# In step 1, one sum of two g blocks by VectorE instead of an accumulating transfer

## The chip, the cores and the metric

The kernel runs on one core of one Trainium2 chip. The metric is the device time of one execution in microseconds. TensorE (PE in the profile) multiplies matrices and writes to PSUM; VectorE (DVE), ScalarE (ACT) and GpSimd (POOL) work element by element; SyncE (SP) and GpSimd issue the transfers. Each engine runs its own instructions in the order in which the program lists them, and waits on semaphores for the others.

## The reference

Input: x of 8 x 4096 x 192, all float32. First a convolution along the sequence with 7 taps, whose weights are a softmax over 8 heads of 24 columns each. Then, for the 32768 rows, two matrix products with an activation between:

```python
h = x @ w_in                                   # 192 -> 2048
g = h * (1.0 / (1.0 + np.exp(-1.702 * h)))
return (g @ w_out).astype(np.float32)          # 2048 -> 192
```

## The kernel before

**Steps.** The rows are cut into 32 steps (`big`, 0 to 31) of 1024 rows: 512 of one batch and 512 of another. Step 0 (`first_step`) is a simple one that runs while the weights are still being prepared. Steps 1 to 31 run the same code: `hidden(big, 0, ...)` and `hidden(big, 1, ...)` compute the first product in two halves, `second(big, ...)` the second product. All of it is written out by hand; nothing is reordered by a scheduler.

**The first product.** Each half multiplies combinations of weight blocks by combinations of the convolved input in a scheme that needs fewer block products than the plain way (`TERMS`, 21 products). The results are combined by VectorE with `sum2` (line 642; one instruction for each half of a PSUM pair, shown as L644) and copied by ScalarE into the buffers k15 to k20. Then ScalarE applies the activation (`gelu`, line 619) and writes `g`. The last combination of a half is `k18 = k18 + sums` (line 746); the last gelu is made of it. `sums` is a pair of PSUM banks.

**g blocks and spots.** g holds 16 blocks of 128 x 1024 numbers, `block(r, j)`, 512 KB each. A `spot` (line 139) is a place for one such block: spots 0 and 1 lie in `osbs` (the output staging buffer), spots 2 to 4 in `room` (the space of k19, k20 and k18), spots 5 to 20 are the g blocks themselves. Blocks of r 0 and 1, spots 5 to 12, come from the first half of the first product, spots 13 to 20 from the second half.

**The second product.** It, too, uses a scheme with fewer block products, and so needs sums of g blocks. `sum_g` (line 929) makes one: either an add or subtract of VectorE (`add_up`, lines 389 to 393; the profile shows L391 for an add, L393 for a subtract), or, with "acc", a transfer issued by GpSimd that adds one spot to another on the way (line 932). `EARLY_G` (line 887) lists the sums that need only the first half's blocks. They are issued in four places (`early(0)` to `early(3)`, lines 692, 700, 715, 733) of the second half (`v` = 1). For spot 8 these are `(0, 5, "+", 6)` on VectorE, into spot 0, and `(8, 0, "acc")`, which adds spot 0 to spot 8; both stand in `early(2)`. `early(3)` holds `(2, 9, "-", 0)`; it stands behind the VectorE sums for k20 and k16 and ahead of the one for k18.

`PLAN` (line 891) is the order of the second product proper. "main" and "side" name a form of the weights, a spot and a target; "go" issues so many steps, each of three matmuls of the main product (column groups 0 to 2) and one of the side product (the fourth column group) (lines 972 to 981; the profile shows L956). "sum" and "acc" are `sum_g`, "seed" and "join" are copies and sums of the small results. Its beginning:

```python
("side", 13, 16, "k0"), ("main", 1, 5, "p2", 1), ("go", 4), ("sum", 14, 14, "-", 18),
("main", 16, 10, "p3", 0), ("go", 2), ("sum", 7, 8, "-", 7), ("go", 1), ("cross",), ("go", 1),
("main", 0, 14, "p0", 1), ("go", 1), ("sum", 5, 11, "-", 19), ("go", 1), ("seed", "p4", "p2", 1),
("go", 1), ("seed", "k1", "p3", 1), ("go", 1), ("sum", 8, 8, "-", 16), ("seed", "p5", "k1", 1),
("side", 19, 1, "k1"), ("acc", 14, 13), ("main", 18, 0, "p2", 0), ("go", 3), ("sum", 6, 8, "-", 6),
("go", 1), ("main", 5, 8, "p1", 0), ("go", 1), ("sum", 4, 5, "-", 10), ...
```

So sums 7, 8 and 6 read spot 8, and so does the fifth main product. The side product goes to `sides = (bx[1], bs[1], by[1])`, one PSUM bank for each third of its columns; `bs` is the pair that the first product calls `sums`.

**Work for later steps.** The convolution of later steps runs beside this. GpSimd adds taps (line 509) and makes the convolution sums (`sums_c`, line 523, shown as L391 and L393 on POOL); it also issues the accumulating transfers of g and of some taps (lines 932, 521), all in one queue. SyncE issues the loads of x (line 99), the transfers that copy conv_t across to the other half of the partitions (`cross`, line 530, shown as L532) and the stores.

In step 1 the second half of the first product carries some work that later steps don't have there: with `big` = 1 the convolution of step 2 is made late, partly in this half (`work`, `turn_next`).

Of the kernel before, what the change touches and what calls it, by code (L numbers as in the profile page):

```python
# [15 lines left out]
def kernel(  # L16
# [546 lines left out]
    def give(early, big):  # L563
        given[early] = big
        for what in waiting[early]:
            cross_now(early, *what)
        waiting[early].clear()
# [44 lines left out]
    def terms(big, v, slot, *ts, first=False):  # L612
        for t in ts:
            product1(slot, *TERMS[t], big, v, first)
            first = False
# [3 lines left out]
    def gelu(b, u, v, src):  # L619
        m, n = divmod(b, 2)  # L620
        i = 2 * (v * len(PAIRS) + PAIRS.index((m, u)))
        dst = g[:, i // NG, n, :, i % NG : i % NG + 2, :]
        if isinstance(src, list):
            for h in range(2):
                act.activation(  # L625
                    dst[:, :, h, :], src[h].rearrange("p (o t) -> p o t", o=2), AF.Gelu_apprx_sigmoid
                )
        else:
            act.activation(  # L629
                dst.rearrange("p o h t -> p h o t"),  # L630
                src.rearrange("p h (o t) -> p h o t", o=2),
                AF.Gelu_apprx_sigmoid,
            )
# [4 lines left out]
    def copy2(dst, src):  # L638
        for h in range(2):
            act.copy(bank(dst, h), bank(src, h))  # L640

    def sum2(op, dst, a, b):
        for h in range(2):
            op(*(bank(t, h) for t in (dst, a, b)))  # L644
# [6 lines left out]
    def hidden(big, v, x, z, y, sums, work, fetch, last=lambda: None):  # L651

        def pe(slot, *ts, first=False):
            terms(big, v, slot, *ts, first=first)

        def taps_at(n):
            for _ in range(0 if v else n):
                next_tap()  # L660

        def early(i):
            for item in EARLY_G[i] if v else ():
                sum_g(*item)


        if v:
            pe(z, 7, first=True)
            give(True, big)
        if v:  # L670
            pe(sums, 12)
            copy2(k15, sums)
            pe(x, 5, 17)
        else:
            pe(x, 5)
            pe(sums, 12)
            copy2(k15, sums)
            pe(x, 17)
            taps_at(1)
        gelu(B11, 0, v, x)  # L680
        if not v:
            pe(z, 7, first=True)
        pe(sums, 0)
        copy2(k16, sums)
        taps_at(2)
        last()
        def turn_next():
            if big + 2 < N_BIG:
                need(f"done {big + 1}")
                turn_x(big + 2)  # L690

        early(0)
        if not v:
            work(2.0 if big > 1 else 1.6)
        elif big == 1:
            work(3.2)

        pe(y, 6, 14, first=True)
        sum2(vec.tensor_sub, x, z, k15)
        early(1)  # L700
        if not v or big == 1:
            work(1.6 if big > 1 else 1.2)
        pe(sums, 13)
        copy2(k19, sums)
        pe(x, 2)
        copy2(k18, x)
        taps_at(2)
        pe(z, 11)
        pe(sums, 20, 10)
        sum2(vec.tensor_sub, k15, y, k19)  # L710
        gelu(B12, 0, v, sums)
        pe(x, 4)
        copy2(k20, x)
        sum2(vec.tensor_sub, k19, z, k19)
        early(2)
        if not v or big == 1:
            work(1.1)
        gelu(B22, 1, v, k19)
        gelu(B22, 0, v, k15)
        taps_at(2)  # L720
        pe(y, 8)
        pe(sums, 1, 9, first=True)
        pe(y, 15)
        if v and big == 1:
            turn_next()
        elif not v:
            work(2.2 if big > 1 else 1.1)
        sum2(vec.tensor_add, k20, k20, sums)
        sum2(vec.tensor_sub, k16, y, k16)
        gelu(B11, 1, v, k20)  # L730
        pe(x, 18)
        gelu(B21, 1, v, x)
        early(3)
        fetch()
        if not v:

            copy2(y, z)
        gelu(B21, 0, v, k16)
        if not v:
            work(1.2)  # L740
        if not v and big > 1:
            turn_next()
        pe(sums, 3, 19)
        if not v:
            work(0.7)
        sum2(vec.tensor_add, k18, k18, sums)
        return lambda: gelu(B12, 1, v, k18)
# [129 lines left out]
    def store(big, n, o=None, queues=(nc.sync,) * 3):  # L877
# [9 lines left out]
    EARLY_G = [  # L887
        [(6, 6, "-", 10)], [(1, 7, "-", 6), (1, 1, "-", 11)], [(0, 5, "+", 6), (8, 0, "acc")],
        [(2, 9, "-", 0)],
    ]  # L890
    PLAN = [
# [37 lines left out]
    def sum_g(dst, a, op, b=None):  # L929

        if op == "acc":
            nc.gpsimd.dma_start(out=spot(dst), in_=spot(a), accum_op=ALU.add)  # L932
        else:
            add_up(spot, dst, a, op, b)
# [3 lines left out]
    def second(big, bx, by, bs, final, last):  # L938
# [66 lines left out]
        )  # L1005
        for item in PLAN:
            ops[item[0]](*item[1:])
# [6 lines left out]
    def work(us):  # L1014
        while todo and todo[0][1] <= us + 0.2:
            us -= todo[0][1]
            todo.pop(0)[2]()

    def next_tap():
        if ready:  # L1020
            ready.pop(0)[2]()
            while ready and ready[0][1] == 0:
                ready.pop(0)[2]()

    def need(label):
        for q in (todo, ready):
            while any(item[0] == label for item in q):
                q.pop(0)[2]()
# [161 lines left out]
    def turn_x(big):  # L1190
        for c in range(NC):
            transpose_x(big, c)
        if big + 1 < N_BIG:
            load_x(big + 1)
# [5 lines left out]
    def fetch(big, v, slot):  # L1200

        need(f"first {big}")
        terms(big, v, slot, 16, first=True)
# [49 lines left out]
```

## Time and profile before

| | us |
|---|---|
| median of 3 runs | 2283.81 (2282.80 to 2284.13) |
| the profiled execution | 2282.62 |
| its span | 2280.6 |
| PE busy | 2267.5 (99%) |
| DVE busy | 1930.9 (85%) |
| ACT busy | 1558.3 (68%) |
| POOL busy | 839.4 (37%) |

The profile is of one execution. Its span runs from the first to the last instruction; the execution's own time is a little more. "L393" is line 393 of the kernel, and a line can be that of a helper that serves many callers. A row of the order of time gives start, duration, engine, line, operation, output, inputs, shapes and count, and in brackets how long the engine had been idle before and what ended that. The chain is the work that ended last, followed back from the end to what released each piece. Step 1's second product starts at about 134 us and step 2's first product at 174.5 us.

### The profile page before, as it was taken

To read this page: it belongs to the slowest core of one execution; us is meant where nothing else is said; L and a number is where in the kernel's file an instruction comes from. 1 tells how busy PE (TensorE), PEld (TensorE's weight loads), DVE (VectorE), ACT (ScalarE), POOL (GpSimd) and SP (SyncE) were. 2 spreads that over 40 slices of the span, in tenths; PEclk is the share of its full clock that TensorE was granted. 3 is DMA by queue.
4 is the path that set the end of the run, shared out by engine and by line. 5 is a ranking of instruction groups with operands and counts; after the bars stand their busy time and mean duration, and the time that the engine had idled before them with its cause. 6 is when DMAs were issued, how large, how long until landed. Compare 5 with 4: busy or idle time off the path is not lost.

```text
span 2280.6 us, 60969 instructions
## 1 busy us (share of the span) xinstructions
PE 2267.5 (99%) x25238; PEld 1196.6 (52%) x25238; DVE 1930.9 (85%) x2794; ACT 1558.3 (68%) x2959; POOL 839.4 (37%) x826
## 2 busy tenths in 40 slices
PE   9999999999999999999999999999999999999999
PEld 5345555555555555555555555555555555555556
DVE  8888888888888888888888888888888888888877
ACT  7657766667766677666776666776667766667754
POOL 0444342344432344424444234443244442344400
PEclk9999999999999999999999999999999999999999
DMA  8866566665567665666656666556756566664443
GB/s 188 155 133 137 114 123 126 126 139 115 110 126 143 124 130 113 127 131 125 137 115 118 126 133 134 119 109 126 143 119 135 111 129 130 123 141 85 91 99 71
DMA packets 269076, 283.94 MB, mean 125 GB/s; under 512 B 117888, under 2 KB 205952, under 8 KB 268672
## 3 DMA queue, kind: packets, MB, share of 16 engines
q0 software_dynamic: 56496, 148.86, 36.4%
q1 hardware_dynamic: 210656, 130.80, 25.4%
q8 instruction: 199, 3.26, 0.6%
q14 instruction: 77, 0.63, 0.1%
q10 hardware_dynamic: 1648, 0.39, 0.1%
HBM read 53.15 MB, written 25.17 MB: 34 GB/s over the span
## 4 chain that ended last, share of the span: by engine, by line
PE 96%; DVE 1%; DMA 1%; POOL 1%; ACT 1%; issue 0%; SPq 0%; DVEq 0%; POOLq 0%; ACTq 0%
PE slot L603 34%; PE slot L956 33%; PE sums L603 15%; PE sums L956 12%; PE slot L802 1%; DMA g<-g 1%; POOL conv_t L509 0%; DMA g<-osbs 0%; DVE conv_t L496 0%; POOL conv_t L393 0%; DVE xt L473 0%; DMA xin<-in_x_dram 0%; DVE w_in_s L391 0%; DVE osbs L874 0%; ACT w_form L435 0%
## 5 line engine op out<-in xcount | busy, mean ns | idle before, releaser
L603 PE MATMUL slot<-conv_t,w_in_s 64*128 64x512 f32 x3740 | 861.1, 591 | 0.6 <-DVE room L644 0.3
L956 PE MATMUL slot<-g,w_form 128*32 128x256 f32 x7024 | 710.3, 379 | 0.0
L603 PEld LDWEIGHTS slot<-conv_t,w_in_s 64*128 64x128 f32 x3740 | 371.4, 187 | 430.3 <-issue 355.0
L393 DVE TENSOR_TENSOR g<-g 128x1024 f32<-128x1024 f32 x372 | 450.1, 1237 | 9.6 <-DMA g<-osbs 6.2
L956 PEld LDWEIGHTS slot<-g,w_form 128*32 128x32 f32 x7024 | 373.0, 110 | 120.3
L603 PE MATMUL sums<-conv_t,w_in_s 64*128 64x512 f32 x1660 | 407.4, 589 | 0.5 <-DVE w_in_s L376 0.3
L981 ACT COPY room<-slot 32x256 f32<-32x256 f32 x434 | 159.4, 367 | 317.0 <-PE slot L956 315.8
L629 ACT ACTIVATE g<-room 128x1024 f32<-128x1024 f32 x310 | 326.0, 1078 | 66.9 <-DVE room L644 66.9
L956 PE MATMUL sums<-g,w_form 128*32 128x256 f32 x2648 | 368.7, 379 | 0.0
L956 PE MATMUL slot<-g,w_out_s 128*32 128x256 f32 x4080 | 320.2, 381 | 5.0 <-DVE g L393 5.0
L932 POOL DMA_DIRECT2D g<-g x124 | 106.3, 857 | 494.7 <-PE sums L956 153.9
L603 PEld LDWEIGHTS sums<-conv_t,w_in_s 64*128 64x128 f32 x1660 | 170.2, 187 | 188.1 <-issue 141.9
L509 POOL TENSOR_TENSOR conv_t<-conv_t,g 128x512 f32<-128x512 f32 x180 | 261.4, 1452 | 15.2 <-POOL conv_t L509 3.9
L521 POOL DMA_DIRECT2D g<-g x120 | 105.6, 880 | 428.5 <-PE slot L956 136.4
L640 ACT COPY room<-slot 128x512 f32<-128x512 f32 x434 | 231.7, 602 | 38.7 <-PE slot L603 38.7
L507 ACT ACTIVATE g<-xt,cw 128x512 f32<-128x512 f32 x360 | 248.8, 731 | 2.2
L956 PEld LDWEIGHTS slot<-g,w_out_s 128*32 128x32 f32 x4080 | 164.9, 110 | 138.1 <-ACT g L625 22.7
L625 ACT ACTIVATE g<-slot 128x512 f32<-128x512 f32 x334 | 180.9, 599 | 49.5 <-PE slot L603 28.8
L496 DVE SCALAR_TENSOR_TENSOR conv_t<-xt,cw,conv_t 128x512 f32<-128x512 f32 (+1 forms) x210 | 194.0, 924 | 10.6 <-ACT conv_t L494 5.9
L956 PEld LDWEIGHTS sums<-g,w_form 128*32 128x32 f32 x2648 | 177.9, 110 | 36.8
L393 POOL TENSOR_TENSOR conv_t<-conv_t 128x256 f32<-128x256 f32 x180 | 181.9, 1025 | 9.4
L981 ACT COPY room<-sums 32x256 f32<-32x256 f32 x217 | 79.6, 367 | 144.3 <-PE sums L956 142.6
(184 smaller groups left out, 2883.4 us busy)
## 6 DMA issues: line engine op xcount, KB each, us to landing
g<-g POOLq DMA_DIRECT2D x124, 512.0 KB, 5.8
xin<-in_x_dram SPq DMA_DIRECT2D x240, 180.0 KB, 4.4
conv_t<-conv_t SPq DMA_DIRECT2D x180, 192.0 KB, 3.2
g<-g POOLq DMA_DIRECT2D x120, 256.0 KB, 3.8
out_dram<-osbs SPq DMA_DIRECT2D x186, 128.0 KB, 4.9
g<-osbs POOLq DMA_DIRECT2D x31, 512.0 KB, 4.7
g<-room POOLq DMA_DIRECT2D x31, 512.0 KB, 5.3
conv_t<-g POOLq DMA_DIRECT2D x60, 256.0 KB, 4.7
```

Of the source, the lines that this page charges most:

```text
L393: eng.tensor_sub(v(dst), v(a), v(b))
L496: vec.scalar_tensor_tensor(out=dst, in0=src, scalar=tap, in1=dst, op0=ALU.mult, op1=ALU.add)
L507: act.mul(home, conv_src(big, c, k), cw[:, c, k : k + 1])
L509: nc.gpsimd.tensor_add(dst, dst, home)
L521: nc.gpsimd.dma_start(out=out, in_=src, accum_op=ALU.add)
L603: nc.tensor.matmul(slot[h], w_in_s[halves[h], a, v * P : (v + 1) * P], src, start=first, stop=True, skip_group_check=True,)
L625: act.activation(dst[:, :, h, :], src[h].rearrange("p (o t) -> p o t", o=2), AF.Gelu_apprx_sigmoid)
L629: act.activation(dst.rearrange("p o h t -> p h o t"), src.rearrange("p h (o t) -> p h o t", o=2), AF.Gelu_apprx_sigmoid,)
L640: act.copy(bank(dst, h), bank(src, h))
L932: nc.gpsimd.dma_start(out=spot(dst), in_=spot(a), accum_op=ALU.add)
L956: nc.tensor.matmul(dst, w, t, start=first, stop=last, skip_group_check=True)
L981: act.copy(to, d)
```

## The change

In step 1 alone, the "acc" of spot 8 leaves `early(2)`, and `early(3)` begins with an add of VectorE, `(8, 8, "+", 0)`, which computes the same sum. All other steps keep `EARLY_G`.

```diff
         def early(i):
-            for item in EARLY_G[i] if v else ():
+            for item in (EARLY_G if big > 1 else EARLY_G_1)[i] if v else ():
                 sum_g(*item)
...
     EARLY_G = [
         [(6, 6, "-", 10)], [(1, 7, "-", 6), (1, 1, "-", 11)], [(0, 5, "+", 6), (8, 0, "acc")],
         [(2, 9, "-", 0)],
     ]
+    EARLY_G_1 = EARLY_G[:2] + [EARLY_G[2][:1], [(8, 8, "+", 0)] + EARLY_G[3]]
```

## The prediction

> **What bounds the kernel now.** I read the page's first lines and its chain by engine, then who TensorE (PE) waited for, then the chain, the clock and each engine's order of time around the one large wait.
>
> ```profile
> PE 2267.5 (99%) x25238; PEld 1196.6 (52%) x25238; DVE 1930.9 (85%) x2794; ACT 1558.3 (68%) x2959; POOL 839.4 (37%) x826
> ...
> PE 96%; DVE 1%; DMA 1%; POOL 1%; ACT 1%; issue 0%; SPq 0%; DVEq 0%; POOLq 0%; ACTq 0%
> ```
>
> TensorE is busy for 99% of the span of 2280.6 us and carries 96% of the chain, so only what lets TensorE run earlier changes the time. Its waits over the whole span, the two largest after start-up:
>
> ```profile
> PE slot L956 <- DVE g L393: 5.0, 1, 5.0
> ...
> PE slot L603 <- DVE room L644: 0.3, 1, 0.3
> ```
>
> The columns are total, times, longest. One wait of 5.0 us stands out; from 165 us to the end the same view has no row, so whatever TensorE gains before 165 us reaches the end unless a new wait takes it. The chain around it (start, us, what):
>
> ```profile
> 132.31 2.35 POOL conv_t L393 x2
> 134.66 7.96 DMA g<-osbs
> ...
> 143.79 2.36 DVE g L393 x2
> ...
> 146.19 1.06 PE slot L956 x5
> ```
>
> "DMA g<-osbs" is the accumulating transfer that the diff removes from step 1. GpSimd (POOL) issues it at 134.66, behind its convolution sums; it lands 7.96 us later; only then can VectorE (DVE) run "sum 7 = 8 - 7", then sum 5, then sum 8, whose result TensorE's fifth main product reads. VectorE in order of time:
>
> ```profile
> 120.24 1.83 DVE L393 TENSOR_TENSOR osbs<-g 128x1024 f32<-128x1024 f32 x1
> 122.18 2.10 DVE L393 TENSOR_TENSOR osbs<-osbs,g 128x1024 f32<-128x1024 f32 x1
> ...
> 132.16 1.28 DVE L393 TENSOR_TENSOR room<-g,osbs 128x1024 f32<-128x1024 f32 x1
> 134.02 1.28 DVE L644 TENSOR_TENSOR room<-room,slot 128x512 f32<-128x512 f32 x2 [0.58 <-PE slot L603]
> 135.22 1.22 DVE L393 TENSOR_TENSOR g<-g 128x1024 f32<-128x1024 f32 x1
> 142.65 4.75 DVE L393 TENSOR_TENSOR g<-g 128x1024 f32<-128x1024 f32 x4 [6.21 <-DMA g<-osbs]
> ```
>
> The row at 132.16 is early sum (2, 9, "-", 0); the new add goes right ahead of it. 134.02 is the two halves of the k18 sum, 135.22 is sum 14, 142.65 is sums 7, 5, 8, 6. GpSimd's operations beside these (the first goes with VectorE's rows at 120.24 and 122.18, the second with the row at 132.16; a further one, alone, takes 0.73 from 133.98):
>
> ```profile
> 121.07 2.13 POOL L509 TENSOR_TENSOR conv_t<-conv_t,g 128x512 f32<-128x512 f32 x1
> ...
> 132.31 1.71 POOL L393 TENSOR_TENSOR conv_t<-conv_t 128x256 f32<-128x256 f32 x1
> ```
>
> The clock, by stretches (us; busy us and instructions of PE, PEld, DVE, ACT, POOL; granted clock; DMA share; GB/s):
>
> ```profile
> 141.20:146.10 4.90, 0.00 (x0) 0.00 (x0) 3.46 (x3) 0.73 (x2) 0.00 (x0) 0.95 1.03 230
> 146.20:149.00 2.80, 2.80 (x28) 1.35 (x32) 2.80 (x3) 0.00 (x0) 0.17 (x1) 0.50 0.75 214
> ```
>
> After the wait TensorE runs 2.8 us at half clock; from 149 us on it is 1.00 again. 0.95 over the first stretch puts the drop at about 4.9 x 0.05 / 0.5 = 0.5 us before its end, some 4.4 us into the wait.
>
> **The change part by part.**
>
> Removed, the wait: sum 7 no longer needs a transfer. The ready time of main product 5 without the wait is 146.19 - 5.04 = 141.15 (the order of time gives the idle as 5.04). New order on VectorE: the two halves of k18, then sums 14, 7, 5, 8 back to back at a pitch of 1.14 us (142.65, 143.79, 144.92 in the trace). If k18 still ended at 135.30, sum 8 would end at 135.22 + 3 x 1.14 + 1.22 = 139.86, ahead of 141.15: all 5.04 us come back.
>
> Removed, the slow clock: 2.8 us at 0.50 do 1.4 us of work. Without an idle stretch of that length the drop goes: 1.40 us. Together 6.44 us.
>
> Removed from GpSimd's queue: one issue of 0.88 us at 134.66 and a 512 KB transfer in a stretch where the DMA engines are full (share 1.03 above). GpSimd's next work, the transfer into block 14, starts at 139.74, when the main product that reads block 14 is done, so it starts no earlier: worth 0. SP's queue (transfers that copy conv_t across, 135.18 to 146.86) is not reordered.
>
> Added on VectorE: one add of two g blocks, 128x1024. It waits for nothing: its source was written by VectorE itself at 126.60, and no engine reads block 8 before the second product. Queued behind it: (2, 9), the k18 sum, sums 14, 7, 5, 8. Alone such an operation costs 1.14 to 1.22 us; k18 had 0.58 us of idle ahead of it, which hides half. But GpSimd runs beside it. In the rows at 120.24 to 123.2 the two engines take turns: VectorE's add ends at 122.07, GpSimd's, begun at 121.07, runs on to 123.20, and VectorE's next, begun at 122.18, ends at 124.28, 1.08 after GpSimd's end. By this pattern: the new add takes the place and the 1.28 us of the row at 132.16, to 133.44; GpSimd's operation of 132.31 runs out to 134.02 as now; (2, 9), next on VectorE, ends at 134.02 + 1.08 = 135.10; k18 starts at 135.02 (VectorE starts 0.08 before the former end, as at 124.20) and ends at 136.30 in place of 135.30. k18 itself has one source in PSUM and took 0.69 us a half beside GpSimd's operation of 133.98, so I give it no such loss.
>
> Who waits for k18: first TensorE. Its second half reads PSUM bank 1 of `sums`, which the second third of the first side product overwrites. That matmul starts with main product 16, at 135.81 now (main 1 starts at 134.04 and its four steps, three matmuls and one of the side product each, take 1.72 us). With 0.05 us from VectorE's end to TensorE's start (146.14 to 146.19) it would start at 136.35: a new wait of 0.54 us. The bounds: with the add at its 1.14 pitch and (2, 9) at 1.28, k18 ends at 135.85 and the wait is 0.09; below nothing is excluded, since the add stands ahead of k18 in a strict order. At the other end both operations take 2.58, the longest 128x1024 row there is (115.93): k18 ends near 138.45, wait 2.7. I take 0.54, because the row at 132.16 is the very slot. Then ScalarE (ACT): the last gelu moves from 135.40 to 136.40, ends at 137.46; its copies of the side product follow at TensorE's pace with over 0.5 us to spare. Sum 14 ends at 137.44 and main 0, moved by 0.54, needs it at 138.05. Sum 8 ends at 140.9, needed at 141.69: 0.8 us to spare, so no second wait. In step 2, with its transfer at 205.62 early enough, the same sums start 1.2 us behind TensorE's second product and nothing waits; here it would be 1.7 us behind.
>
> GpSimd's last convolution sum starts at 135.1 and ends at 135.8 in place of 134.7; SP's copies behind it land by 154 to 155. They are wanted by step 2's first product at 174.5 - 5.9 = 168.6: hidden by 13 us.
>
> The Trainium skill ("SBUF — State Buffer", Who interferes with whom) says that a VectorE instruction with two SBUF inputs and a GpSimd instruction that reads SBUF exclude each other, the later one fully blocked; the rows at 120 to 124 us agree, and this is the rule that speaks against the change. By it the sum is the 5.9 below, without it 6.35.
>
> Sum: 5.04 + 1.40 - 0.54 = 5.90 us. The profiled execution took 2282.62 (span 2280.6 and 2.0 around it) and would take 2276.7. It lies 1.2 below the median of the runs shown, 2283.81; from that, **2277.9 us**.
>
> **The rivals.**
>
> (a) The add hides: GpSimd's operation yields and the new wait is 0.09. For it: k18's 0.58 idle. Against: the turns at 120 to 124. 2283.81 - 6.35 = 2277.5.
>
> (b) Both VectorE operations wait as long as the row at 115.93: gain 6.44 - 2.7 = 3.7, 2280.1. Against: only 0.73 us operations run on GpSimd then, while that row waited for one of 1.75.
>
> (c) The new 0.54 wait brings the half clock by itself: gain 5.90 - 1.40 = 4.5, 2279.3. Against: the 0.3 wait at 131 did not, the 5.04 wait did after 4.4 us. The Trainium skill ("TensorE: Matmul & The Clock Gate", Part 1) puts the drop after an idle window of about 3.4 us; by that rule 0.54 is far too short, and no row here lies between 0.3 and 5.0.
>
> (d) The change doesn't do what it says: another arrival held sum 7 until about 142.6 and the transfer was only the last. DMA is full there, but sum 7 reads blocks 8 and 7, and 7 was written by VectorE: little for it. 2283.8.
>
> (e) Slower: GpSimd's convolution sums, blocked by the added add, delay the copies of conv_t so far that step 2's first product waits. That begins only when they land 13 us later than worked out and ends above the old time after 19; at 24 it gives 2289. The rows give GpSimd a delay of 1.1.
>
> **How the numbers follow.** The forecast 0.66; (a) 0.18, (b) 0.05, (c) 0.04, (d) 0.04, (e) 0.03. About 0.2%, 4.6 us, can be told from no change here; the line lies at 2279.2. Faster: forecast and (a), 0.84. Within: (b), (c), (d), 0.13. Slower: (e), 0.03. The range runs from (a) on the lowest run shown (2282.8 - 6.4 = 2276.4) up to (b), 2280.1; outside lie (d), (e) and some spread.
>
> **What would show it.** Right: no wait of TensorE on "DVE g L393"; no half clock near 146; the row of four sums joined to the one at 135; a small new wait, "DVE room L644", at 135.8 of about 0.5; (2, 9) stretched to about 1.7; no "DMA g<-osbs" at 134.7. Wrong: a wait above 2 us at 135 to 142, a half clock after it, or a wait of "PE slot L603" on conv_t near 168.

## The result and the profile after

The changed kernel takes 2276.71 us in the median of 7 runs (2276.07 to 2276.84); the kernel before, beside it, 2283.81 (2282.80 to 2286.19, 7 runs). The ratio is 0.9968, interval 0.9956 to 0.9979: faster by 0.32%, and the whole interval lies beyond the 0.2% that the prediction took as its line. Forecast were 2277.9 us with a range of 2276.4 to 2280.1. The profiled execution took 2276.84 with a span of 2274.8; the prediction put it at 2276.7.

The page of the kernel after:

```profile
span 2274.8 us, 60966 instructions
...
PE 2266.5 (100%) x25238; PEld 1208.8 (53%) x25238; DVE 1944.9 (85%) x2795; ACT 1556.9 (68%) x2959; POOL 836.8 (37%) x825
```

One VectorE instruction more, one GpSimd instruction fewer, and TensorE at 100% of the span where it was at 99%. Whom TensorE waited for in the whole span (total us, times, longest), the first rows:

```profile
PE sums L455 <- POOL osbs masks.py:199: 1.4, 1, 1.4
PE slot L1044 <- DVE xt L473: 0.5, 1, 0.5
PE slot L603 <- DVE room L644: 0.5, 1, 0.5
```

The row of 5.0 us "PE slot L956 <- DVE g L393" is gone and nothing of its size has come. The "DVE room L644" row is the one that was there with 0.3, at 131 us, not k18. The view puts it down to the k20 sum, which ends at 131.30:

```profile
131.43 1.09 PE L603 MATMUL slot<-conv_t,w_in_s 64*128 64x512 f32 x3 [0.51 <-DVE room L644]
```

But SyncE's copy of conv_t, which the first matmuls for step 2 read inside step 1's first product, lands at 131.30 too. TensorE starts 0.13 us after that; where a wait ends with VectorE beyond doubt (k18 in `repeat1` and `repeat3`) it starts 0.05 to 0.06 after it, and where one ends with this copy (`acc_first`, and the second profile of the kernel before) 0.14. By these delays the wait is the copy's, in the first profile of the kernel before as well (0.14 after VectorE's sum, 0.13 after the copy). The clock in the two stretches that were idle and half speed before (columns as in the prediction):

```profile
141.20:146.10 4.90, 4.90 (x99) 4.84 (x93) 4.90 (x6) 1.69 (x5) 0.86 (x1) 1.00 1.02 222
146.20:149.00 2.80, 2.80 (x60) 2.77 (x53) 2.77 (x3) 1.10 (x5) 1.16 (x2) 1.00 1.07 240
```

TensorE is busy throughout, at clock 1.00. VectorE in order of time, and below it GpSimd's:

```profile
132.43 1.30 DVE L391 TENSOR_TENSOR g<-g,osbs 128x1024 f32<-128x1024 f32 x1
133.65 1.75 DVE L393 TENSOR_TENSOR room<-g,osbs 128x1024 f32<-128x1024 f32 x1
135.32 1.27 DVE L644 TENSOR_TENSOR room<-room,slot 128x512 f32<-128x512 f32 x2
136.51 5.88 DVE L393 TENSOR_TENSOR g<-g 128x1024 f32<-128x1024 f32 x5
```

```profile
131.10 4.88 POOL L393 TENSOR_TENSOR conv_t<-conv_t 128x256 f32<-128x256 f32 x4
140.21 0.90 POOL L933 DMA_DIRECT2D g<-g  x1 [4.22 <-DVE g L393]
```

The first row is the new add. (2, 9) behind it is stretched to 1.75, GpSimd's four sums take 4.88 where they took 3.90, k18 ends at 136.59, and the five sums follow without a gap. All of this stands 0.26 us later than in the profile of before, as step 1's second product does (134.30 instead of 134.04).

Where the time went is best read by step. The table gives, for each profile, the time from the first matmul of step 1's first product (L603) to that of its second product (L956, 957 after the change), and from there to the first matmul of step 2's first product. All are starts in the order of time. From step 2 on the second product takes 33.80 to 33.81 us in every profile here but that of `all_steps`; "loss" is what step 1 takes above it, to 0.01 us.

| kernel | step 1, first product | step 1, second product | loss | span |
|---|---|---|---|---|
| before | 49.89 | 40.43 | 6.63 | 2280.6 |
| after | 50.06 | 34.41 | 0.61 | 2274.8 |

The period of steps 2 to 31 is 70.058 us in both, and from step 2 on both take 2106.1 us. So the gain of the profiled pair, 5.77 us, is the loss that went (6.02) less variations of a tenth or two elsewhere.

### The profile page after: what moved, and what is told of

Its sections match the earlier page's. It is cut to its first block, busy times and chain, and to the rows that moved or that the text cites. A ratio compares the mean times of both kernels' runs of the same rounds, so it can differ in the third digit from the quotient of the medians.

```text
span 2274.8 us, 60966 instructions
## 1 busy us (share of the span) xinstructions
PE 2266.5 (100%) x25238; PEld 1208.8 (53%) x25238; DVE 1944.9 (85%) x2795; ACT 1556.9 (68%) x2959; POOL 836.8 (37%) x825
## 4 chain that ended last, share of the span: by engine, by line
PE 99%; ACT 0%; DVE 0%; DMA 0%; issue 0%; SPq 0%; DVEq 0%; ACTq 0%
PE slot L603 35%; PE slot L957 34%; PE sums L603 16%; PE sums L957 13%; PE slot L802 2%; DMA xin<-in_x_dram 0%; DVE xt L473 0%; ACT conv_t L1062 0%; DVE conv_t L496 0%; SPq L99 0%; ACT conv_t L357 0%; DVE room L644 0%; ACT conv_t L356 0%; DVE osbs L874 0%; ACT w_form L435 0%
## 5 line engine op out<-in xcount | busy, mean ns | idle before, releaser
L603 PE MATMUL slot<-conv_t,w_in_s 64*128 64x512 f32 x3740 | 861.1, 591 | 0.8 <-DVE room L644 0.5
L603 PEld LDWEIGHTS slot<-conv_t,w_in_s 64*128 64x128 f32 x3740 | 372.0, 187 | 429.9 <-issue 354.3
L393 DVE TENSOR_TENSOR g<-g 128x1024 f32<-128x1024 f32 x372 | 454.3, 1248 | 3.4 <-ACT g L629 0.2
L603 PE MATMUL sums<-conv_t,w_in_s 64*128 64x512 f32 x1660 | 407.5, 589 | 0.5 <-DVE w_in_s L376 0.3
L603 PEld LDWEIGHTS sums<-conv_t,w_in_s 64*128 64x128 f32 x1660 | 170.5, 187 | 187.8 <-issue 141.6
L496 DVE SCALAR_TENSOR_TENSOR conv_t<-xt,cw,conv_t 128x512 f32<-128x512 f32 (+1 forms) x210 | 198.9, 947 | 10.6 <-ACT conv_t L494 5.9
L393 POOL TENSOR_TENSOR conv_t<-conv_t 128x256 f32<-128x256 f32 x180 | 183.8, 1034 | 9.4
```

Source lines behind the costliest of these rows:

```text
L393: eng.tensor_sub(v(dst), v(a), v(b))
L496: vec.scalar_tensor_tensor(out=dst, in0=src, scalar=tap, in1=dst, op0=ALU.mult, op1=ALU.add)
L603: nc.tensor.matmul(slot[h], w_in_s[halves[h], a, v * P : (v + 1) * P], src, start=first, stop=True, skip_group_check=True,)
```

## The experiments

### Without the sum

```diff
-    EARLY_G_1 = EARLY_G[:2] + [EARLY_G[2][:1], [(8, 8, "+", 0)] + EARLY_G[3]]
+    EARLY_G_1 = EARLY_G[:2] + [EARLY_G[2][:1], EARLY_G[3]]
```

> Step 1 leaves out the sum of spot 8 altogether: neither the transfer nor the add (step 1's output is then not the reference's). Theory (the add costs a small new wait through k18): without it k18 ends 1.0 us earlier, TensorE no longer waits at main product 16, sum 8 is ready before main product 5; the time lies 0.3 us (as the trace of after has it) to 0.5 us below the changed kernel, near 2276.3. Rival (the add is hidden wholly): the same 2276.7. Rival (the transfer's wait was not the only thing that held sum 7): a wait of several us before main product 5 stays, 2280 or more.

Measured: 2275.65 us (2275.25 to 2276.76, 5 runs); second product of step 1 33.81, loss 0.01. VectorE in order of time:

```profile
131.42 1.29 DVE L393 TENSOR_TENSOR room<-g,osbs 128x1024 f32<-128x1024 f32 x1
133.28 1.28 DVE L644 TENSOR_TENSOR room<-room,slot 128x512 f32<-128x512 f32 x2 [0.57 <-PE slot L603]
134.48 5.88 DVE L393 TENSOR_TENSOR g<-g 128x1024 f32<-128x1024 f32 x5
```

k18 starts with 0.57 us of idle ahead of it, as before the change, and with no transfer to wait for the five sums follow at once. Nothing else had held sum 7: rival (d) falls. The add as placed costs 0.61 - 0.01 = 0.60 us of step 1's second product, a little more than the 0.3 to 0.5 expected. The time, from another chip, agrees with that in sign but is not the measure of it: of the 1.6 us between the two spans, 0.8 lies in step 1's first product (49.27 against 50.06), where the changed kernel's profile has the wait of 0.5 us at 131, ahead of the add, and this one has none.

### The add where the transfer stood

```diff
-    EARLY_G_1 = EARLY_G[:2] + [EARLY_G[2][:1], [(8, 8, "+", 0)] + EARLY_G[3]]
+    EARLY_G_1 = EARLY_G[:2] + [EARLY_G[2][:1] + [(8, 8, "+", 0)], EARLY_G[3]]
```

> The changed kernel with the add in early(2), right behind (0, 5, +, 6), where the transfer was issued, in place of early(3). Theory (VectorE is in order and the place decides): the add now stands ahead of the transposes of x and of the k20 sum, for which TensorE already waits 0.5 us at about 131 us; that wait grows by 1.1 to 1.7 us, while the wait at main product 16 shrinks or goes; 2277.5 to 2278.2, no half clock. Rival (the place does not matter, VectorE has room): 2276.7 with the same two waits.

Measured: 2276.95 us (2276.51 to 2278.11, 5 runs), below the expected 2277.5 to 2278.2. In the profiled execution, the slowest of the five, TensorE waits 1.2 us for the k20 sum, and the loss in the second product fell to 0.14. That is the exchange that was expected, but no wait grew by 1.1 to 1.7: the 0.5 at 131 us in the changed kernel is the copy's, which lands early here (129.91), and the 1.2 is new. TensorE in order of time:

```profile
133.53 2.58 PE L603 MATMUL slot<-conv_t,w_in_s 64*128 64x512 f32 x8 [1.21 <-DVE room L644]
```

So the place only chooses which of two waits is paid. In the median both places come out within 0.3 us of each other, which these runs can't tell apart.

### The transfer kept, but issued earlier

```diff
     def sums_c(big, i):
+        if big == 2 and i and 0 not in held:
+            held.append(i)
+            return
         add_up(
...
                 sum_g(*item)
+            if v and big == 1 and i == 2:
+                late = [j for j in held]
+                held.append(0)
+                for j in late:
+                    sums_c(2, j)
```

> The kernel before, transfer kept, no add; in step 1 alone GpSimd's convolution sums 1 to 7 for step 2 are issued behind the transfer in place of ahead of it, so the transfer is issued about 128.5 instead of 134.7. Theory (what made TensorE wait is that the transfer stands late in GpSimd's queue, behind the convolution sums): it lands at 133.5 to 136.5, sum 7 waits little or not at all, no half clock; 2276.0 to 2277.5. Rival (the transfer itself, in full DMA engines, is what is slow): it takes 10 us or more and TensorE still waits 2 us or more; 2279 or more. Rival (the convolution sums issued later hold up step 2): a new wait near 168 to 175 us.

Measured: 2281.63 us (2275.40 to 2283.24, 10 runs, three of them below 2275.6). TensorE in order of time, then GpSimd's row of the transfer, in the profiled execution (2283.24):

```profile
135.88 5.50 PE L608 MATMUL slot<-conv_t,w_in_s 64*128 64x512 f32 x12 [4.65 <-DMA conv_t<-conv_t]
```

```profile
129.53 0.90 POOL L942 DMA_DIRECT2D g<-osbs  x1
```

Issued at 129.53 instead of 134.66, the transfer no longer delays anyone: the second product loses 0.01 us. That much of the theory holds: it was late because it stood behind the convolution sums. But the first product takes 56.76 us where it took about 50. TensorE waits 4.65 us, and at half clock after it, for SyncE's copy of conv_t (chain: issued at 130.11, 5.63 us to landing), the copy of the wait at 131 us. None of the three expectations had this wait. In the first profile of the kernel before, the same copy was issued at 128.98 and took 2.06 us, with the DMA engines at a share of 0.32; here they were full meanwhile (1.04 from 131.0 to 134.3). That the copy lands late because the transfer now shares the DMA engines with it is my reading, and was not tested by itself. In three runs the time is as low as without the sum, which suggests that the race for this copy is sometimes won; none of the three was profiled.

### The add in all steps

```diff
-            for item in (EARLY_G if big > 1 else EARLY_G_1)[i] if v else ():
+            for item in EARLY_G_1[i] if v else ():
```

> The add of VectorE in place of the transfer in all steps 1 to 31. Theory: in later steps TensorE never waited for the transfer, and GpSimd runs no sums beside early(3), so the add costs VectorE 1.2 us a step in front of a k18 sum that has 0.6 us of idle ahead of it and 0.3 us before TensorE needs its bank; 0 to 0.3 us a step: 2276.7 to 2286, likeliest 2278 to 2281. Rival (VectorE has room everywhere): 2276.7 within 0.5. Rival (fewer transfers relieve the DMA engines): below 2276.

Measured: 2280.94 us (2280.45 to 2281.75, 11 runs), 4.2 above the changed kernel. Its step period is 70.193, longer by 0.135 in each later step; the part from step 2 on takes 2110.84 instead of 2106.1. Thirty periods make 4.05 us of that, and the other 0.7 lies in the last step, where TensorE waits 0.4 us for k18. VectorE in step 3:

```profile
271.82 1.28 DVE L644 TENSOR_TENSOR room<-sums,room 128x512 f32<-128x512 f32 x2
273.02 1.21 DVE L391 TENSOR_TENSOR g<-g,osbs 128x1024 f32<-128x1024 f32 x1
274.15 1.22 DVE L393 TENSOR_TENSOR room<-g,osbs 128x1024 f32<-128x1024 f32 x1
275.29 1.27 DVE L644 TENSOR_TENSOR room<-room,slot 128x512 f32<-128x512 f32 x2
```

With no GpSimd sum beside them the add costs a pitch of 1.13 us, of which 0.61 was idle time ahead of k18 and most of the rest slack behind it; 0.135 remains. That is the add without taking turns; in step 1 of the changed kernel it costs 0.60.

The turns alone don't set that cost, though. Step 1 here is the changed kernel's own, so this is a third profile of it, and in it GpSimd's sums were over at 132.61:

```profile
132.66 1.20 DVE L391 TENSOR_TENSOR g<-g,osbs 128x1024 f32<-128x1024 f32 x1
133.78 1.21 DVE L393 TENSOR_TENSOR room<-g,osbs 128x1024 f32<-128x1024 f32 x1
134.91 1.27 DVE L644 TENSOR_TENSOR room<-room,slot 128x512 f32<-128x512 f32 x2
```

No turns, and yet the second product takes 34.81 us, a loss of 1.01. The copy of conv_t, which waits for an earlier sum of GpSimd, had landed at 129.06 and not held TensorE, which began the second product at 133.49; k18 ended 2.70 us after that. In the two profiles of the changed kernel k18 ends 2.29 and 2.24 us after that start, in the later steps here 1.82, in `repeat1` 3.86; each time the loss is what goes beyond 1.69 us. The cost is set by how far k18 ends behind TensorE's start, and the turns are one way to lengthen that.

### k18 later still

The first kernel writes (2, 9) twice in step 1, the second four times, with the same values:

```diff
-    EARLY_G_1 = EARLY_G[:2] + [EARLY_G[2][:1], [(8, 8, "+", 0)] + EARLY_G[3]]
+    EARLY_G_1 = EARLY_G[:2] + [EARLY_G[2][:1], [(8, 8, "+", 0)] + EARLY_G[3] * 2]
```

> The changed kernel with (2, 9, -, 0) written twice in step 1 (the same values again), so that k18 ends later by one more VectorE operation beside GpSimd's last sum, 1.1 to 1.8 us. Theory (k18's bank is what TensorE waits for, and a wait of about 2 us does not bring the half clock): TensorE's wait at main product 16 grows by 1.1 to 1.8 us, step 1 by the same, no half clock; 1.1 to 1.8 us above the changed kernel. Rival (half clock after shorter waits too): 1.4 us more than that, with a half clock in the trace. Rival (k18 is not what TensorE waits for): the time of the changed kernel.

```diff
-    EARLY_G_1 = EARLY_G[:2] + [EARLY_G[2][:1], [(8, 8, "+", 0)] + EARLY_G[3]]
+    EARLY_G_1 = EARLY_G[:2] + [EARLY_G[2][:1], [(8, 8, "+", 0)] + EARLY_G[3] * 4]
```

> As repeat1, but (2, 9, -, 0) four times: k18 ends 3.4 to 4.1 us later than in the changed kernel, and TensorE's wait at main product 16 is 4.0 to 4.7 us. Theory (a wait of this length brings the half clock in some executions or all, by where it falls): 3.4 to 4.1 us above the changed kernel without it, up to 1.7 us more with it, so 2280.1 to 2282.5. Rival (the half clock of before had to do with the transfer and not with the idle time): no half clock, 2280.1 to 2280.8 in all executions.

Measured: 2278.01 us (2277.66 to 2278.59, 10 runs) with two, 2282.24 (2281.55 to 2283.23, 10 runs) with four: 1.3 and 5.5 above the changed kernel. The losses of step 1 are 2.17 and 6.30. TensorE's longest wait, with two and with four:

```profile
PE slot L957 <- DVE room L644: 1.6, 1, 1.6
```

```profile
PE slot L957 <- DVE room L644: 4.2, 1, 4.2
```

The clock around the second (columns as above):

```profile
130.00:138.00 8.00, 5.92 (x55) 3.01 (x51) 7.90 (x8) 2.98 (x4) 5.08 (x5) 1.00 1.00 226
138.00:142.00 4.00, 1.91 (x20) 0.99 (x24) 4.00 (x5) 1.42 (x2) 0.00 (x0) 0.72 0.83 211
142.00:146.00 4.00, 4.00 (x69) 2.62 (x61) 3.97 (x5) 1.72 (x5) 0.84 (x1) 0.85 0.42 114
```

Both waits end on k18, so k18's bank is what TensorE meets first when VectorE is late. The wait of 1.6 us brought no half clock; that of 4.2 did, with no transfer in the case, for 4 x 0.28 / 0.5 + 4 x 0.15 / 0.5 = 3.4 us. TensorE starts again at 140.1, so the half clock costs it about 1.5. Of the 6.30 lost, 4.2 is the wait, 1.5 the half clock, and the rest, like 0.6 of the 2.17 before, is loss that no idle time shows.

The first profile also shows the turns from the other side. GpSimd's sums were early there (129.86, four in 2.91 us, done at 132.77), and the add and both copies of (2, 9) ran unhindered:

```profile
132.81 1.20 DVE L391 TENSOR_TENSOR g<-g,osbs 128x1024 f32<-128x1024 f32 x1
133.93 2.47 DVE L393 TENSOR_TENSOR room<-g,osbs 128x1024 f32<-128x1024 f32 x2
```

### The add behind k18

```diff
+            if big == 1 and item[:2] == ("sum", 7):
+                sum_g(8, 8, "+", 0)
             ops[item[0]](*item[1:])
...
-    EARLY_G_1 = EARLY_G[:2] + [EARLY_G[2][:1], [(8, 8, "+", 0)] + EARLY_G[3]]
+    EARLY_G_1 = EARLY_G[:2] + [EARLY_G[2][:1], EARLY_G[3]]
```

> The changed kernel with the add moved out of early(3), to the second product, right ahead of sum 7 and behind k18 and sum 14. Theory (the add costs 0.6 us only because it stands ahead of k18): k18 ends as without the add, TensorE's wait at main product 16 goes; sum 8 ends 1.14 us later, 0 to 0.2 us behind TensorE's need of it; step 1 shorter by 0.4 to 0.6 us, 2276.1 to 2276.3. Rival (the sums behind it are as tight, so the wait only moves to main product 5): 2276.7 or more.

Measured: 2276.14 us (2275.74 to 2276.70, 6 runs). VectorE in order of time:

```profile
134.48 1.28 DVE L644 TENSOR_TENSOR room<-room,slot 128x512 f32<-128x512 f32 x2 [0.58 <-PE slot L603]
135.68 1.22 DVE L393 TENSOR_TENSOR g<-g 128x1024 f32<-128x1024 f32 x1
136.82 1.22 DVE L391 TENSOR_TENSOR g<-g,osbs 128x1024 f32<-128x1024 f32 x1
138.07 4.76 DVE L393 TENSOR_TENSOR g<-g 128x1024 f32<-128x1024 f32 x4
```

k18 is on time again, and the loss of step 1 is 0.22 instead of 0.61. Since 0.4 us is little, the two ran beside each other on one chip:

> The changed kernel unchanged, beside add_in_plan_2 on one chip. Theory (with the transfer gone, step 1 has nothing left that varies by us): times within 1 us of each other, near 2276.7; step 1's second product 0.1 to 0.7 us longer than the 33.80 of later steps, the more the longer GpSimd's sums run beside the add. Rival (the copy of conv_t that TensorE waited 1.3 us for in one profile of the kernel before varies by itself): times spread over 2 us or more.

> add_in_plan once more, on the chip of after_again. Theory: 0.3 to 0.6 us below after_again in the median. Rival (the difference of the former runs was one of chips): within 0.2 us of it.

Measured: 2276.67 us (2276.16 to 2277.29, 6 runs) for the changed kernel, 2276.51 (2275.95 to 2276.54, 5 runs) for this one, 0.9968 and 0.9966 of the kernel before. The losses in the profiles are 0.55 and 0.22. The trace shows 0.3 to 0.4 us, in two pairs of profiles; but the medians differ by 0.16 only, under the 0.3 to 0.6 expected, and the times overlap and can't tell the two kernels apart. The changed kernel's times lie within 1.2 us of each other, a little more than expected.

### The kernel before, three more profiles

No edit; the kernel before as it is.

> The kernel before, unchanged, profiled once more. Theory (its time varies by up to 9 us from execution to execution because the wait on the transfer does, as its landing falls): the time from step 2 on is 70.06 us a step as in the other profiles, and what differs in the span from 2280.6 lies in the wait for the transfer in step 1, with the half clock behind it. Rival (the variation lies in start-up or is spread over the steps): the wait is 5.0 us again with another span.

> The kernel before, profiled again. Theory (the transfer's wait and the half clock behind it vary): step 1's second product takes 37 to 42 us, against 33.80 in later steps, and together with any wait for the copy of conv_t this accounts for the difference of its span from the other profiles of before to 0.5 us. Rival: the difference lies in the start-up or in later steps.

> A further profile of the kernel before. Theory: step 1's second product takes 37 to 42 us again and accounts for the span to 0.5 us; rival: start-up or later steps differ.

Measured, with the first profile and the transfer's time from issue to landing:

| profile | transfer | TensorE's wait | half clock | second product | loss | span |
|---|---|---|---|---|---|---|
| first | 8.0 | 5.0 | 3.4 | 40.43 | 6.63 | 2280.6 |
| second | 8.5 | 5.6 | 6.8 | 41.40 | 7.60 | 2282.4 |
| third | 9.5 | 6.5 | 6.8 | 42.78 | 8.98 | 2282.2 |
| fourth | 9.3 | 6.4 | 6.8 | 41.95 | 8.15 | 2282.7 |

The third one's waits and clock:

```profile
PE slot L956 <- DVE g L393: 6.5, 1, 6.5
```

```profile
146.00:149.00 3.00, 2.01 (x20) 0.99 (x24) 2.97 (x3) 0.00 (x0) 0.00 (x0) 0.50 0.60 151
149.00:151.00 2.00, 2.00 (x24) 0.96 (x20) 1.71 (x3) 0.28 (x1) 0.86 (x1) 0.50 0.00 1
151.00:153.00 2.00, 2.00 (x40) 1.03 (x36) 2.00 (x3) 0.14 (x2) 0.40 (x1) 0.87 1.06 203
```

TensorE starts again at 147.0 and runs at half clock to about 151.5: 4.5 us, 2.25 lost, on top of a wait of 6.5. The later the transfer lands, the longer the wait, and the half clock may last 3.4 or 6.8 us. From step 2 on all four take 2106.1 us. The second product doesn't account for the span alone, though: the first product of step 1 varies too, from 49.26 (third) to 50.90 (second), with the wait for the copy of conv_t that `acc_first` ran into: 1.3 us in the second, 0.4 in the fourth, 0.3 in the first, none in the third. The second products differ from the first profile's by 1.0, 2.35 and 1.5 us, the first products by 1.0, -0.6 and 0.1, the spans by 1.8, 1.65 and 2.1. So the theory that it is step 1 and not the later steps holds, with two waits and not one: the remaining -0.1, -0.1 and 0.5 us lie ahead of step 1.

## Why the prediction was right

**The removed wait and the slow clock (6.44 us).** Right. Both went whole. In the first profile they were 6.63: counted from start to start of matmuls the wait is 0.2 longer than the 5.04 of idle time that I read, because a matmul's record goes on beyond the next one's start. `no_sum` shows that nothing stood behind them, and `repeat3` that the half clock belongs to the idle time.

**The new wait (0.54).** Right in place, and in size in the changed kernel's own two profiles: losses of 0.61 and 0.55. In the third profile of the same code, step 1 of `all_steps`, it is 1.01. The turns were as worked out: add 1.30 (1.28 expected), (2, 9) 1.75 (ends 1.09 after GpSimd's), k18 ending at 136.59 - 0.26 = 136.33 in the first profile's time (136.30 expected). One sign failed: I had expected a row "DVE room L644" at 135.8 among the waits. There is none; three column groups went on with their matmuls while the fourth waited (sets of four start every 0.2 us up to 135.83, two sets of three at 136.05 and 136.26, the next of four at 136.64, 0.05 after k18's end), so the view has no idle time, and the loss is seen only in the length of the second product. At 1.6 us, in `repeat1`, the row appears.

**What was costed at nothing.** GpSimd's next transfer starts at 140.21, released by the main product as before: 5.91 us into the second product, where it was 5.70. (The row names a sum of VectorE, but none of these writes or reads the blocks of this transfer, 14 and 13, but sum 14, done at 137.73.) SyncE's copies, behind GpSimd's later sums, held nobody: no wait near 168 us, so rival (e) falls. Rival (a) falls in the changed kernel's own two profiles, but the turns depend on where GpSimd's sums fall, which varies: in `repeat1` and `all_steps` they were over before the add began. Even then (a)'s wait of 0.09 doesn't come: in `all_steps` it is 1.01. The prediction moved k18's end and held TensorE's start fixed; but the copy of conv_t, which holds TensorE, waits for an earlier sum of GpSimd, and where it lands early TensorE needs k18's bank earlier. So the size is partly luck: in the changed kernel's two profiles the copy held TensorE by 0.5 us, much as it did by 0.3 in the profile that the 0.54 was worked out from. Rivals (b) and (c) fall: the longest stretch was 1.75, and waits up to 1.6 brought no half clock. Two readings were a little off and change nothing: the bound of (a) comes out at 135.78 for k18's end and no wait, if VectorE's overlap of 0.08 is counted there as it is elsewhere, and in step 2 the sums start 1.30 us behind TensorE, not 1.2.

**The forecast of 2277.9 was 1.2 us high.** The mechanism and the profiled execution's sum were right (2276.7 forecast, 2276.84 measured). What was mis-sized is the term "removed wait and slow clock" when it was carried over to the median of the kernel before: I took 6.44 off 2283.81, but 6.44 belongs to an execution with the shortest wait of the four profiled ones. The three others lost 7.6 to 9.0. The kernel before varies from 2277.3 to 2287.0 us over its runs on all chips, the changed kernel from 2276.1 to 2277.3; the loss went with its spread.

## What to carry to other kernels

A wait that varies from run to run is worth its mean, not what one profile shows; if the new path has no such wait, set the forecast from the profiled execution's own time less its loss, not from the median less it. When an in-order engine takes over work, look at what stands right behind the new instruction and when the next engine needs that: here 0.6 us of idle time ahead of k18 hid half of the add, and behind k18 the add loses only 0.2. Where a transfer is late because of its place in a queue, moving it forward can make another transfer the late one, as in the profile of `acc_first`.

## What the runs showed of the hardware

The half clock came in two lengths, 3.4 and 6.8 us, after waits of 4.2 to 6.5 us, and not after 1.6. The Trainium skill ("TensorE: Matmul & The Clock Gate", Part 1) gives windows of about 3.4 us that run freely; both lengths are multiples of that. The length of the wait doesn't tell which one comes: 4.2 and 5.0 brought the short one, 5.6 to 6.5 the long one, and 4.65 in `acc_first` the long one too. What goes with it in these six profiles is how soon after the drop TensorE works again:

| profile | wait | clock drops, after the wait's start | TensorE works again, after the drop | half clock |
|---|---|---|---|---|
| `repeat3` | 4.2 | 3.9 | 0.3 | 3.4 |
| before, first | 5.0 | 4.5 | 0.6 | 3.4 |
| `acc_first` | 4.65 | 3.1 | 1.6 | 6.8 |
| before, third | 6.5 | 4.3 | 2.3 | 6.8 |
| before, second | 5.6 | 2.4 | 3.2 | 6.8 |
| before, fourth | 6.4 | 2.7 | 3.7 | 6.8 |

The drop came 2.4 to 4.5 us into the wait, so the 4.4 that the prediction read from one profile is near the late end of what these six show.

VectorE's adds of two blocks in SBUF and GpSimd's sums took turns, one instruction each, when both had work: four instructions in turn at 132.4 to 136.0 us in the changed kernel, where a GpSimd sum of 0.73 alone took 1.71 and a VectorE operation of 1.2 took 1.75.
